# Loading Wq in one transfer instead of two, with the order of the lead-in written anew

## The chip, the cores and the metric

One core of one Trainium2 chip. The time is the device time of one execution in microseconds (us); a kernel's time is the median of several executions. Besides the times there is one profiled execution, whose trace gives the start and length of each instruction on TensorE (PE, its weight loads PEld), VectorE (DVE), ScalarE (ACT), GpSimd (POOL) and the queue of SyncE (SP), which issues the DMAs here.

## The reference

A layer norm, then a sliding dilated attention (32 heads of 16, window 8, dilation 2) and a gated feed-forward side by side, added to the input. S = 2048 rows, D = 512, Df = 1376, all bf16.

```python
xn  = layernorm(x)                                # over the 512 columns
qkv = xn @ wqkv                                   # 512 x 1536: q, k, v
k, v at positions s, s-2, ..., s-14               # masked where negative
o   = softmax(q . k * 16**-0.5) . v               # per head, 8 positions
att = o @ wo
h   = gelu(xn @ w_gate) * (xn @ w_up)             # 512 x 1376 each
out = x + att + h @ w_down
```

## The kernel before

The rows are worked in four blocks of 512 (b = 0 to 3), each of four tiles of 128 rows (t = 0 to 15). Input loads bring pairs of tiles (p = 0 to 7): ld_x0 and ld_x1 as two loads of 128 rows each, the others as one load of 256 rows. Everything stays in SBUF; all weights are loaded once.

The program is a graph of named tasks (`G.task`, with the items that each reads and writes) and an order per engine written out by hand in `ORDER`, a string of task names for each of pe, act, dve, pool and sp. `schedule` walks these orders and gives buffers and PSUM banks (8 of them, pool `ps`) to the tasks, and `assign_sync` sets semaphore waits for what a task reads, overwrites or needs freed. Each engine then executes its list strictly in order: a task that waits holds up all behind it on its engine. On SP that holds for DMA issues: an issue that waits for an event keeps later ones from being issued. The durations in `PARAMS` and in the tasks (`nbytes` too) serve only that walk through the orders; they emit nothing.

What happens in the lead-in, for block 0:

- ld_x0_0, ld_x0_1, Wq in two halves (ld_wq0: rows 0 to 255, ld_wq1: rows 256 to 511, 256 KB each, L652), ld_x1_0, ld_wk, ld_x1_1, ld_wv (L646, 512 KB each), ld_x2, ld_x4, ld_x3, then ld_wg0 and ld_wu0 (L664, 1280 KB each), where ld_wg0 is made to wait until ld_wk has landed. ld_x3 and ld_x5 wait for a slot of XIN that the transposes of pair 0 and pair 1 on TensorE free.
- Norms: statistics (bnst, bnag), square root (sq, on ScalarE), reciprocal (rstd), sub and norm, for tiles 0 to 7 on VectorE. Tile 1 has its sums on ScalarE (sx1, negm1, sxx1, sq1).
- Transposes of block 0 on TensorE (tpx, tpy), evicted to xnT by evx (ScalarE) and evy (VectorE, half of tiles 0 and 1). For block 1 they are DMA transposes: trx2_0, trx2_1, trx3_0 and trx3_1 (L864), tiles 4 to 7, each after the norm of its tile (norm4 to norm7).
- Q of tiles 0 and 1: mma0_t takes the first two of the four slices of 128 rows of Wq (they are in ld_wq0) and mmb0_t the last two (ld_wq1), both L970. Then K of tile t is mmt1_t, Q of tiles 2 and 3 mmt0_t (L956), V mmv (L1014); evicted by evq0, evk0, evv0 on ScalarE.
- Feed-forward of block 0: fg0_j and fu0_j (L1259: Wg and Wu), evicted by gelu0_j and uev0_j. The last 96 columns lie in Wt, loaded by ld_wt0, ld_wt1, ld_wt2 (L671).
- Attention of block 0: products q.k on VectorE (pr0_0, pr0_1, L1070), summed (pa0), reduced per head on TensorE by er0_3 (L1106, a part of the feed-forward with Wt, and L1113), masked (L1136), evicted by lc0 (L1142), exponent, and so on. Block 1's products are mm1_w_g_0 (w = 0, 1, 2 for q, k, v; L1039); the first, mm1_0_0_0, needs all four DMA transposes of block 1.

The lines of the load of Wq, as they are before:

```python
if i == 0:
    for h in range(2):
        ...
                Wqkv[:, 2 * h:2 * h + 2, 0:512],
                A_wqkv[256 * h:256 * h + 256, 0:512].rearrange("(k p) n -> p k n", p=128))
        t_w = G.task("sp", "ld_wq%d" % h, 0, mk(), wr=[(I_wq, ("q", h))], ...)
```

Of the kernel before, what the change touches and what calls it, by code (L numbers as in the profile page):

```python
# [96 lines left out]
class Graph:  # L97
# [250 lines left out]
    def report(self):  # L348
# [14 lines left out]
ORDER = {  # L363
    "pe":
        "warm0 warm1 warm2 warm3 warm4 warm5 warm6 warm7 warm8 warm9 tpx0_0 tpy0_0 warm10 warm11 warm12 "
        "warm13 warm14 mma0_0 tpx0_1 tpy0_1 mmb0_0 mma0_1 mmb0_1 mmt1_0 tpx1_0 mmt1_1 mmt1_2 tpx1_1 mmt0_2 "
        "mmv0_1 mmt1_3 mmt0_3 mmv0_0 mmv1_0 fg0_0 fg0_1 fg0_2 fg0_3 fu0_0 fg0_4 fu0_1 fu0_2 fu0_3 mm1_0_0_0 "
        "fu0_4 mm1_1_0_0 fg0_5 mm1_1_1_0 fu0_5 er0_3 mm1_0_1_0 fg0_6 mm1_2_3_0 fg1_0 mm1_0_2_0 mm1_1_2_0 "
        "mm1_0_3_0 mm1_1_3_0 fu1_0 fg0_7 fu0_6 fu0_7 fg1_1 fu1_1 fg0_10 fg0_8 fg1_2 fu1_2 fg1_3 mm1_2_2_0 "
        "fu1_3 fg0_9 fg1_4 mmv1_1 fu1_4 fu0_8 fu0_9 er1_3 fg1_5 mm1_2_0_0 fg1_6 fu1_5 fg1_7 fg1_8 fu1_6 fg1_9 "  # L370
# [6 lines left out]
        "fg3_9 fu3_8 fu3_9 acca8 accb8 accd11 acca12 accd15_1 accd9 accb12 accd13 accd14_0 accd10 accd15_0 "  # L377
        "accw13 accw15_1 accw15_0 accw12 accd14_1 accw14_0 accw14_1 accd15_2 accw15_2",
    "act":
        "c_tbl sx1 sq0 negm1 sxx1 evx0_0 sq1 evx0_1 sq2 evq0_0 evq0_1 evx1_0 sq3 evk0_1 evk0_0 bnst8 evx1_1 "  # L380
        "evk0_2 sq4 evq0_2 bnst9 sq6 evk0_3 ve8 evq0_3 vp8 bnag8 evv0_1_0 bnag9 evv0_0_1 sub9 gelu0_1 bnst10 "
        "bnst11 gelu0_0 uev0_0 ve10 gelu0_3 vp10 evv0_0_0 uev0_3 va8 gelu0_2 vb8 evq1_0_0 bnag10 evk1_0_0 "
        "uev0_4 uev0_2 bnag11 uev0_1 va10 halo1 bnst12 evk1_1_0 vb10 lc0 evq1_1_0 uev0_5 gelu0_5 gelu0_6 "
        "gelu0_4 exp0 evq1_2_0 evv1_3_0 evq1_3_0 bnst13 evk1_3_0 ln0 d5_0 evk1_2_0 gelu1_0 sub10 uev0_6 "
        "gelu1_1 uev1_1 uev1_0 sub8 uev0_10c ve12 uev0_10a uev0_10b uev0_7 norm8 gelu0_10 gelu0_8 sub11 "
# [10 lines left out]
        "uev2_9 uev3_6 gelu3_6 gelu3_7 gelu2_8 uev3_10a gelu3_10 uev3_7 uev3_9 gelu3_9 fe8 gelu3_8 uev3_8 "  # L396
        "fe11 fe9 fe10 fe13 fe12",
    "dve":
        "c_wdz bnst0 bnag0 sub0 rstd0 norm0a norm0b mean1 sub1 evy0_0 rstd1 norm1a norm1b evy0_1 bnst2 bnag2 "
        "sub2 rstd2 norm2 bnst3 bnag3 sub3 rstd3 norm3 bnst4 bnst5 bnag4 bnag5 bnst6 bnst7 bnag6 rstd4 sub5 "  # L400
        "bnag7 sub4 sub7 norm5 rstd6 norm4 sub6 norm7 norm6 pr0_1 pr0_0 pa0 h0_1 mask h0_0 rstd8 d1a_0 d1b_0 "
        "d1c_0 d2_0 pr1_0 d4a_0 rstd10 d4b_0 d4c_0 h0_2 d6_0 pr1_1 h1_0 pa1 h0_10 pb1 h0_3 pv0_1 d1a_1 h1_1 "
        "h0_4 d1b_1 pv0_0 d1c_1 h1_2 d2_1 h1_3 pw0_1 d4a_1 pw0_2 d4b_1 pz0 d4c_1 pr2_0 rstd12 d6_1 pr2_1 "
        "h1_10 fin3 h1_4 pa2 fin0 rstd14 pb2 pv1_0 d1a_2 fin1 d1b_2 pv1_1 d1c_2 d2_2 pw1_1 d4a_2 d4b_2 h2_1 "
# [4 lines left out]
        "c_ones c_onef c_id c_vnpad c_idb c_eps c_mhalf c_e8a c_e8b c_e8c c_e8d c_ktpad c_mask0 c_mask1 c_utz "  # L409
        "sq8 sq10 sq12 sq14",  # L410
    "sp":
        "ld_x0_0 ld_x0_1 ld_wq0 ld_wq1 ld_x1_0 ld_wk ld_x1_1 ld_wv ld_x2 ld_x4 ld_x3 ld_wg0 ld_wu0 ld_x5 "
        "ld_wt0 trx3_0 trx3_1 trx2_1 trx2_0 ld_x6 ld_wt1 ld_wt2 ld_wd0 ss0_0 ss0_3 ss0_1 ss0_2 ld_wd1 ld_x7 "
        "sl0_3 ld_wo sl0_2 ldxr1 ldxr3 sl0_0 trx4_0 sl0_1 trx5_1 trx5_0 trx4_1 ss1_1 ss1_0 ss1_2 ss1_3 sl1_0 "
        "ldxr0 trx6_1 sl1_1 sl1_2 sl1_3 ldxr2 trx7_1 trx6_0 trx7_0 ss2_2 ss2_3 ldxr8 sto1 ss2_1 ldxr9 ss2_0 "
        "sto3 sl2_0 sl2_1 ldxr4 ldxr11 sl2_3 sl2_2 ldxr7 ldxr5 sto4 ldxr15 sto2 ldxr14 ss3_1 ss3_2 ldxr6 "
        "ss3_3 ss3_0 ldxr12 ldxr10 ldxr13 sto0 sl3_1 sl3_0 sl3_2 sl3_3 sto7 sto5 sto11 sto8 sto9 sto6 sto10 "
        "sto15_1 sto13 sto15_0 sto12 sto14_0 sto14_1 sto15_2",
}


# [16 lines left out]
def bass_parallel_sum__sliding_local_dilated__glu_gated_geglu__prompt_kernel(nc, A_x, A_wqkv, A_wo, B_x, B_w_gate, B_w_up, B_w_down, out, dbg=None, cfg=None):  # L438
# [43 lines left out]
    with contextlib.ExitStack() as es:  # L482
        block = es.enter_context(nc.Block())

        def sb(name, shape, dt):
            return es.enter_context(nc.sbuf_tensor(name, shape, dt))

        Wqkv = sb("Wqkv", [128, 4, 1536], BF)
# [11 lines left out]
        mask = sb("mask", [32, 2, 4, 16], F32)  # L500
# [43 lines left out]
        G = Graph()  # L544
# [20 lines left out]
        I_wq = Item("Wqkv")  # L565
# [51 lines left out]
               prio=PC2)  # L617
        G.task("pool", "c_vnpad", 0.15, lambda e: e.memset(VN[:, VNI[0].slot, :, 0:16], 0.0), wr=[(VNI[0], "pad")],
               prio=PC2)
# [12 lines left out]
        for i, wn in enumerate(WARM[0] + WARM[1]):  # L632
# [6 lines left out]
            t_w = G.task("pe", "warm%d" % i, wn / 1200 if i < len(WARM[0]) else d_mm(wn), mk_w(), wr=[it_warm], prio=-400, mode="f")  # L639
# [4 lines left out]
        for i, nm in enumerate(("q", "k", "v")):  # L644
            def mk(i=i):
                return lambda e: e.dma_start(  # L646
                    Wqkv[:, :, i * 512:(i + 1) * 512],
                    A_wqkv[:, i * 512:(i + 1) * 512].rearrange("(k p) n -> p k n", p=128))
            if i == 0:
                for h in range(2):  # L650
                    def mk(h=h):
                        return lambda e: e.dma_start(  # L652
                            Wqkv[:, 2 * h:2 * h + 2, 0:512],
                            A_wqkv[256 * h:256 * h + 256, 0:512].rearrange("(k p) n -> p k n", p=128))
                    t_w = G.task("sp", "ld_wq%d" % h, 0, mk(), wr=[(I_wq, ("q", h))], prio=-958 + 0.1 * h,
                                 nbytes=480 * 1024)
                continue
            t_w = G.task("sp", "ld_w" + nm, 0, mk(), wr=[(I_wq, nm)],
                         prio=(-958, -957.5, -898)[i], nbytes=512 * 1024)
            t_ld["w" + nm] = t_w  # L660
        I_wt = Item("Wt")
        for (nm, Wx, I_w, src) in (("g", Wg, I_wg, B_w_gate), ("u", Wu, I_wu, B_w_up)):
            def mk(Wx=Wx, src=src):
                return lambda e: e.dma_start(Wx[:, :, :], src[:, 0:1280].rearrange("(k p) n -> p k n", p=128))  # L664
            t_w = G.task("sp", "ld_w%s0" % nm, 0, mk(), wr=[I_w], prio=R_WG + (nm == "u"), nbytes=1280 * 1024)
            t_w.deps.add(t_ld["wk"])
            t_ld[nm] = t_w
        for (i, src, c0, c1, o) in ((0, B_w_gate, 1280, 1376, 32), (1, B_w_up, 1280, 1312, 0),
                                    (2, B_w_up, 1312, 1376, 128)):
            def mk(src=src, c0=c0, c1=c1, o=o):  # L670
                return lambda e: e.dma_start(Wt[:, :, o:o + c1 - c0],  # L671
                                             src[:, c0:c1].rearrange("(k p) n -> p k n", p=128))
            t_w = G.task("sp", "ld_wt%d" % i, 0, mk(), wr=[(I_wt, i)], prio=R_WG + 2 + i, nbytes=2 * (c1 - c0) * 1024)
            G.order_after(t_w, t_ld["u"])
            t_ld["u"] = t_w
        t_w = G.task("sp", "ld_wd0", 0, lambda e: e.dma_start(
            Wd[:, 0:10, :], B_w_down[0:1280, :].rearrange("(j p) n -> p j n", p=128)),
            wr=[(I_wd, 0)], prio=R_WD, nbytes=2000 * 1024)
# [4 lines left out]
        t_w = G.task("sp", "ld_wo", 0, lambda e: e.dma_start(Wo[:, :, :], A_wo.rearrange("(p q) n -> p q n", q=4)),  # L683
                     wr=[I_wo], prio=R_WD + 2, nbytes=512 * 1024)
# [8 lines left out]
        for p in range(NP):  # L693
# [55 lines left out]
            for ts in (((2 * p,), (2 * p + 1,)) if b == 0 else ((2 * p, 2 * p + 1),)):  # L749
                t, n = ts[0], len(ts)  # L750
# [715 lines left out]
```

## Time and profile before

| | us |
|---|---|
| median of 3 runs | 184.42 (184.01 to 185.21) |
| the profiled execution | 184.79 |
| its span, first to last instruction | 182.7 |
| TensorE busy / idle in the span | 177.2 / 5.5 |
| VectorE busy | 169.0 |
| ScalarE busy | 131.8 |

The granted TensorE clock is full throughout. Three kinds of view are read below. The chain of waits goes back from the last instruction to what released each step, and shows in order of time which engine or DMA set the end. A timeline lists the instructions of one engine by start time and, in brackets, how long the engine stood idle before and what ended that. For SP, a row is the time in which an issue occupied the queue, not the transfer itself; a transfer's time to landing is listed apart, counted from the start of its issue:

| load | issued at | us to landing | KB |
|---|---|---|---|
| ld_x0_0 | 0.80 | 2.1 | 128 |
| ld_wq0 | 1.71 | 3.2 | 256 |
| ld_wq1 | 2.19 | 3.4 | 256 |
| ld_x1_0 | 2.70 | 3.4 | 128 |
| ld_wk | 3.21 | 6.0 | 512 |
| ld_x1_1 | 3.69 | 6.0 | 128 |
| ld_wv | 4.23 | 6.9 | 512 |
| ld_wg0 | 9.27 | 8.9 | 1280 |
| ld_wu0 | 9.68 | 11.7 | 1280 |
| ld_x5 | 12.65 | 9.5 | 256 |
| trx3_0, trx3_1 | 16.97, 18.62 | 5.9, 4.8 | |
| trx2_1, trx2_0 | 20.96, 22.27 | 3.1 | |
| ld_x6 | 23.66 | 2.9 | 256 |
| ld_wt1, ld_wt2 | 24.22, 24.77 | 2.6, 4.2 | 32, 64 |

### The profile page before, as it was taken

The page shows a single profiled execution, that of the slowest core. Times are in us where ns is not written, and L with a number is a line of the kernel's source. Part 1 is how long each engine was busy: PE and PEld are TensorE (multiplying, and loading weights), DVE is VectorE, ACT ScalarE, POOL GpSimd, SP SyncE. Part 2 cuts the span into 40 slices and gives each one's busy share as a digit, 9 for nine tenths or more (in the row PEclk, how much of TensorE's full clock was granted, in tenths as well). Part 3 has the DMA queues.
Part 4 walks back from the last instruction along what each step waited for, and adds up shares of the span by engine and source line. Part 5 has one row for each costly group of instructions (what it writes and reads, how often), then busy time and mean ns, then how long its engine had stood idle before and what let it go on. Part 6 is the DMA issues. An engine that isn't in the chain of part 4 may idle for free.

```text
span 182.7 us, 2780 instructions
## 1 busy us (share of the span) xinstructions
PE 177.2 (97%) x1060; PEld 90.5 (50%) x1060; DVE 169.0 (92%) x157; ACT 131.8 (72%) x270; POOL 17.4 (10%) x23
## 2 busy tenths in 40 slices
PE   7799999999999999999999999999999999999994
PEld 2598445444454445444445444444444444454574
DVE  3779997699999999989999999999999999999953
ACT  5569989999999999999387598844268679411030
POOL 6000006200000000974000000000000000000000
PEclk9999999999999999999999999999999999999999
DMA  4999968001794200002572000528105058410113
GB/s 149 299 365 397 141 136 287 2 0 33 171 292 103 57 4 0 0 0 59 144 221 40 0 0 0 125 64 255 47 0 148 1 112 249 127 57 4 57 44 99
DMA packets 26236, 19.60 MB, mean 107 GB/s; under 512 B 13840, under 2 KB 23024, under 8 KB 26224
## 3 DMA queue, kind: packets, MB, share of 16 engines
q1 hardware_dynamic: 26224, 19.44, 39.2%
q8 instruction: 8, 0.13, 0.3%
q14 instruction: 4, 0.03, 0.1%
HBM read 14.71 MB, written 3.15 MB: 98 GB/s over the span
## 4 chain that ended last, share of the span: by engine, by line
PE 55%; ACT 22%; DMA 8%; DVE 6%; POOL 5%; issue 2%; SPq 1%; DVEq 0%
PE PS L1351 23%; PE PS L1259 21%; PE PS L1039 9%; DMA Wg<-in_B_w_gate_dram 5%; POOL sq L803 5%; ACT UU L1276 4%; ACT GG L1269 4%; DMA Wqkv<-in_A_wqkv_dram 3%; DVE UNI L1070 2%; ACT XIN L824 2%; DVE UNI L1082 2%; ACT L1164 1%; ACT EX L1165 1%; ACT PB L1142 1%; ACT KT L1050 1%
## 5 line engine op out<-in xcount | busy, mean ns | idle before, releaser
L1351 PE MATMUL PS<-Wd,HT 128*128 128x512 bf16 (+2 forms) x209 | 40.7, 345 | 0.0
L1259 PE MATMUL PS<-xnT,Wg 128*128 128x512 bf16 x160 | 39.3, 379 | 0.3 <-DMA Wg<-in_B_w_gate_dram 0.3
L1259 PE MATMUL PS<-xnT,Wu 128*128 128x512 bf16 x160 | 39.4, 379 | 0.0
L1221 DVE TENSOR_TENSOR UNI<-VN,PT 128x8192 f16<-128x8192 bf16 x8 | 35.4, 4420 | 0.0
L1070 DVE TENSOR_TENSOR UNI<-QT,KT 128x8192 f16<-128x8192 bf16 x8 | 35.3, 4419 | 0.0
L1039 PE MATMUL PS<-xnT,Wqkv 128*128 128x512 bf16 x144 | 34.7, 379 | 0.1
L1351 PEld LDWEIGHTS PS<-Wd,HT 128*128 128x128 bf16 x209 | 19.7, 98 | 19.4
L1276 ACT ACTIVATE UU<-PS 128x512 bf16<-128x512 f32 x40 | 23.2, 607 | 6.4 <-PE PS L1259 6.3
L1384 ACT ACTIVATE OB<-PS 128x512 bf16<-128x512 f32 x14 | 8.3, 595 | 23.2 <-PE PS L1351 23.1
L1259 PEld LDWEIGHTS PS<-xnT,Wg 128*128 128x128 bf16 x160 | 15.1, 98 | 19.8 <-ACT UU L1276 0.8
L1259 PEld LDWEIGHTS PS<-xnT,Wu 128*128 128x128 bf16 x160 | 15.6, 98 | 18.6 <-ACT KT L1050 0.3
L1039 PEld LDWEIGHTS PS<-xnT,Wqkv 128*128 128x128 bf16 x144 | 16.2, 114 | 15.6 <-ACT UT L1314 0.6
L1269 ACT ACTIVATE GG<-PS 128x512 bf16<-128x512 f32 x40 | 23.0, 608 | 0.5 <-DVE HT L1283 0.4
L803 POOL TENSOR_TENSOR sq<-ve,mhalf 128x2 bf16<-128x2 f32 x4 | 14.6, 3642 | 68.3 <-ACT ve L799 68.3
L1082 DVE TENSOR_TENSOR UNI<-UNI 128x8192 f16<-128x8192 f16 x4 | 17.7, 4420 | 0.0
L1230 DVE TENSOR_TENSOR UNI<-UNI 128x8192 f16<-128x8192 f16 x4 | 17.7, 4420 | 0.0
L1351 PE MATMUL PS<-Wo,OT 128*128 128x512 bf16 (+2 forms) x76 | 16.3, 345 | 0.0
L1283 DVE TENSOR_TENSOR HT<-GG,UU 128x1024 bf16<-128x1024 bf16 x20 | 13.5, 684 | 0.2 <-ACT UU L1276 0.2
L1351 PEld LDWEIGHTS PS<-Wo,OT 128*128 128x128 bf16 x76 | 6.9, 98 | 6.4 <-DVE OT L1241 0.5
L1236 DVE TENSOR_TENSOR UNI<-UNI 128x4096 f16<-128x4096 f16 x4 | 9.1, 2286 | 0.0
L1050 ACT ACTIVATE KT<-PS 128x512 bf16<-128x512 f32 x12 | 7.2, 601 | 2.0 <-PE PS L1039 2.0
L1050 ACT ACTIVATE VN<-PS 128x512 bf16<-128x512 f32 x12 | 7.2, 597 | 1.0 <-PE PS L1039 0.9
(99 smaller groups left out, 179.2 us busy)
## 6 DMA issues: line engine op xcount, KB each, us to landing
PT<-pt_scratch SPq DMA_DIRECT2D x16, 256.0 KB, 4.0
out_dram<-OB SPq DMA_DIRECT2D x14, 128.0 KB, 1.8
XIN<-in_A_x_dram SPq DMA_DIRECT2D x12, 128.0 KB, 2.7
XIN<-in_A_x_dram SPq DMA_DIRECT2D x6, 256.0 KB, 6.8
Wg<-in_B_w_gate_dram SPq DMA_DIRECT2D x1, 1280.0 KB, 8.9
Wu<-in_B_w_up_dram SPq DMA_DIRECT2D x1, 1280.0 KB, 11.7
Wd<-in_B_w_down_dram SPq DMA_DIRECT2D x1, 1280.0 KB, 7.2
Wqkv<-in_A_wqkv_dram SPq DMA_DIRECT2D x2, 512.0 KB, 6.5
```

The costliest lines, as they stand in the source:

```text
L803: "pool", "sq%d" % t, 5.0, lambda e, t=t, n=n: e.tensor_tensor(out=sq[:, t:t + n], in0=ve[:, t:t + n], in1=mhalf[:, 0:n], op=ALU.pow),
L1039: ins = e.matmul(PS[:, 512 * it.slot:512 * it.slot + 512], lhsT=wcols(which, kt, g), rhs=xnT[:, itx.slot, kt, :], start=(kt == 0), stop=(k ...
L1050: return e.activation(out=o, in_=PS[:, 512 * it.slot:512 * it.slot + 512], func=ACTF.Identity, scale=(QSC, 1.0, 1.0)[which])
L1070: return lambda e: e.tensor_tensor(out=UNI[:, it.slot:it.slot + 2, :, :], in0=bass.AP(QT, (itq.slot * 4 + 2 * h) * 512, [[NQT * 4 * 512, 1 ...
L1082: return lambda e: e.tensor_tensor(out=UNI[:, i0.slot:i0.slot + 2, :, :], in0=UNI[:, i0.slot:i0.slot + 2, :, :], in1=UNI[:, i1.slot:i1.slo ...
L1221: return lambda e: e.tensor_tensor(out=bass.AP(UNI, ito.slot * 4096, [[NUNI * 4096, 128], [2048, 4], [512, 4], [1, 512]]), in0=bass.AP(VN, ...
L1230: return lambda e: e.tensor_tensor(out=UNI[:, i0.slot:i0.slot + 2, :, :], in0=UNI[:, i0.slot:i0.slot + 2, :, :], in1=UNI[:, i1.slot:i1.slo ...
L1259: ins = e.matmul(PS[0:M, 512 * it.slot:512 * it.slot + 512], lhsT=Wx[:, kt, j * 128:j * 128 + M], rhs=xnT[:, itx.slot, kt, :], start=(kt = ...
L1269: return lambda e: e.activation(out=GG[:, ito.slot, q, :], in_=PS[:, 512 * it.slot:512 * it.slot + 512], func=ACTF.Gelu_apprx_tanh)
L1276: return lambda e: e.activation(out=UU[:, ito.slot, q, :], in_=PS[:, 512 * it.slot:512 * it.slot + 512], func=ACTF.Identity)
L1283: return lambda e: e.tensor_tensor(out=HT[:, ito.slot, j - 1:j + 1, :], in0=GG[:, ig.slot, :, :], in1=UU[:, iu.slot, :, :], op=ALU.mult)
L1351: ins = e.matmul(PS[:, 512 * it.slot:512 * it.slot + CW], lhsT=(OT[:, ito.slot, q, ti * 128:(ti + 1) * 128] if kind == "o" else HT[:, ith. ...
```

## The change

Wq comes in one load of all 512 rows, in the form that Wk and Wv have already. The load writes both parts of the item that mma and mmb read, so all four of mma0_0, mma0_1, mmb0_0 and mmb0_1 now wait for the whole.

```diff
-            if i == 0:
-                for h in range(2):
...
-                            Wqkv[:, 2 * h:2 * h + 2, 0:512],
-                            A_wqkv[256 * h:256 * h + 256, 0:512].rearrange("(k p) n -> p k n", p=128))
-                    t_w = G.task("sp", "ld_wq%d" % h, 0, mk(), wr=[(I_wq, ("q", h))], prio=-958 + 0.1 * h,
-                                 nbytes=480 * 1024)
-                continue
-            t_w = G.task("sp", "ld_w" + nm, 0, mk(), wr=[(I_wq, nm)],
-                         prio=(-958, -957.5, -898)[i], nbytes=512 * 1024)
+            t_w = G.task("sp", "ld_w" + nm, 0, mk(), wr=[(I_wq, (nm, 0)), (I_wq, (nm, 1))] if i == 0 else [(I_wq, nm)],
+                         prio=(-958, -957.5, -898)[i], nbytes=(900 if i == 0 else 512) * 1024)
```

The orders differ in their first parts alone: TensorE's 27th to 43rd task, ScalarE's 6th to 43rd, VectorE's 14th to 44th, SP's first 22. All tasks behind these stand as before (GpSimd's order is the same throughout). The parts that differ, cut where they are equal; the line breaks of the strings are moved:

```diff
 pe:   ... mmt1_0 tpx1_0 mmt1_1
-      mmt1_2 tpx1_1 mmt0_2 mmv0_1 mmt1_3 mmt0_3 mmv0_0 mmv1_0 fg0_0 fg0_1 fg0_2 fg0_3 fu0_0 fg0_4 fu0_1 fu0_2 fu0_3
+      mmt0_2 tpx1_1 mmt1_2 mmv0_1 mmt0_3 mmt1_3 mmv0_0 mmv1_0 fg0_0 fg0_1 fg0_2 fg0_3 fu0_0 fu0_1 fu0_2 fu0_3 fg0_4
       mm1_0_0_0 fu0_4 mm1_1_0_0 fg0_5 mm1_1_1_0 fu0_5 er0_3 ...
 act:  c_tbl sx1 sq0 negm1 sxx1
-      evx0_0 sq1 evx0_1 sq2 evq0_0 evq0_1 evx1_0 sq3 evk0_1 evk0_0 bnst8 evx1_1 evk0_2 sq4 evq0_2 bnst9 sq6 evk0_3
-      ve8 evq0_3 vp8 bnag8 evv0_1_0 bnag9 evv0_0_1 sub9 gelu0_1 bnst10 bnst11 gelu0_0 uev0_0 ve10 gelu0_3 vp10
-      evv0_0_0 uev0_3 va8 gelu0_2
+      sq1 evx0_0 evx0_1 sq2 evq0_0 evq0_1 evx1_0 sq3 evk0_0 evk0_1 bnst8 evx1_1 bnst9 sq4 evk0_2 ve8 sq6 evq0_2
+      vp8 evq0_3 evk0_3 bnag8 evv0_0_1 bnag9 evv0_1_0 sub9 gelu0_0 bnst10 bnst11 uev0_0 va8 gelu0_3 gelu0_1 ve10
+      gelu0_2 vp10 evv0_0_0 uev0_3
       vb8 evq1_0_0 bnag10 ...
 dve:  ... rstd1 norm1a norm1b
-      evy0_1 bnst2 bnag2 sub2 rstd2 norm2 bnst3 bnag3 sub3 rstd3 norm3 bnst4 bnst5 bnag4 bnag5 bnst6 bnst7 bnag6
-      rstd4 sub5 bnag7 sub4 sub7 norm5 rstd6 norm4 sub6 norm7 norm6 pr0_1 pr0_0
+      bnst2 bnag2 evy0_1 sub2 rstd2 norm2 bnst3 bnag3 sub3 rstd3 norm3 bnst5 bnst4 bnst6 bnag5 bnag4 bnag6 bnst7
+      sub4 bnag7 rstd4 sub6 sub7 rstd6 norm4 norm7 sub5 norm6 norm5 pr0_0 pr0_1
       pa0 h0_1 mask ...
 sp:   ld_x0_0 ld_x0_1
-      ld_wq0 ld_wq1 ld_x1_0 ld_wk ld_x1_1 ld_wv ld_x2 ld_x4 ld_x3 ld_wg0 ld_wu0 ld_x5
-      ld_wt0 trx3_0 trx3_1 trx2_1 trx2_0 ld_x6 ld_wt1 ld_wt2
+      ld_wq ld_x1_0 ld_wk ld_x1_1 ld_wv ld_x2 ld_x4 ld_x3 ld_wg0 ld_wu0 ld_x5
+      trx3_1 ld_wt0 trx3_0 ld_wt1 ld_wt2 trx2_1 trx2_0 ld_x6
       ld_wd0 ss0_0 ...
```

With the orders the PSUM banks that many tasks use change their numbers, since `schedule` hands them out as it goes.

## The prediction

> **What bounds the kernel now.** First the page's list of busy time, which says that TensorE has almost no room:
>
> ```profile
> PE 177.2 (97%) x1060; PEld 90.5 (50%) x1060; DVE 169.0 (92%) x157; ACT 131.8 (72%) x270; POOL 17.4 (10%) x23
> ```
>
> Of the span of 182.7 us, TensorE is idle for 5.5. An edit of the lead-in can win only from the part of those 5.5 us that lies in the lead-in, and loses whatever idle time it adds. Next the chain of waits in order of time (start, length, what):
>
> ```profile
> 3.21 6.05 DMA Wqkv<-in_A_wqkv_dram
> ...
> 9.27 8.87 DMA Wg<-in_B_w_gate_dram
> 18.14 0.05 issue
> 18.19 7.94 PE PS L1259 x36
> 26.14 0.86 PE PS L1039 x4
> ...
> 31.86 0.89 PE PS L1113 x16
> ```
>
> The Wk load (ld_wk) lands at 9.26, Wg lands at 18.14, and from 18.19 TensorE runs without a gap to the logits er0_3 (L1113); VectorE's mask at 32.85 and ScalarE's lc0 at 33.17 take over from there. Further on the chain is ScalarE to 72.6, GpSimd's power (L803) to 81, and TensorE from 95 to 180. So a shift of TensorE between 18 and 32 us goes into the end one for one. Then TensorE's own timeline, for where its idle time is:
>
> ```profile
> 6.61 1.53 PE L970 MATMUL PS<-xnT,Wqkv 128*128 128x128 bf16 x24
> 9.30 1.08 PE L956 MATMUL PS<-xnT,Wqkv 128*128 128x128 bf16 x16 [1.17 <-DMA Wqkv<-in_A_wqkv_dram]
> ...
> 18.19 3.63 PE L1259 MATMUL PS<-xnT,Wg 128*128 128x512 bf16 x16 [0.28 <-DMA Wg<-in_B_w_gate_dram]
> ```
>
> The Q products of the first two row tiles (L970, what the split of Wq feeds) end at 8.13. TensorE then waits 1.17 us for Wk and later 0.28 us for Wg. Last the SP queue, which issues every transfer:
>
> ```profile
> 1.71 0.94 SPq L652 DMA_DIRECT2D Wqkv<-in_A_wqkv_dram  x2
> 2.70 0.47 SPq L702 DMA_DIRECT2D XIN<-in_A_x_dram  x1
> 3.21 0.43 SPq L646 DMA_DIRECT2D Wqkv<-in_A_wqkv_dram  x1
> ...
> 9.27 0.37 SPq L664 DMA_DIRECT2D Wg<-in_B_w_gate_dram  x1
> ...
> 13.06 0.47 SPq L671 DMA_DIRECT2D Wt<-in_B_w_gate_dram  x1
> 16.97 6.57 SPq L864 DMA_TRANSPOSE xnT<-XIN  x4
> 23.66 0.51 SPq L708 DMA_DIRECT2D XIN<-in_A_x_dram  x1
> 24.22 1.05 SPq L671 DMA_DIRECT2D Wt<-in_B_w_up_dram  x2
> ```
>
> One issue costs about 0.5 us; a DMA transpose of a row tile costs 1.60, 2.30, 1.27 and 1.27 us for the four in turn.
>
> **What the Trainium skill says.** "DMA: Bandwidth & Descriptors", section "Queues, rings and completion order": each DMA engine consumes a queue's descriptors in ring order. The trace agrees: in the list of issues with their time to landing, all come from SP and land in order (halves of Wq at 4.9 and 5.6, x1_0 at 6.1, Wk at 9.2, x1_1 at 9.7, Wv 11.1, Wg 18.14, Wu 21.4). The same page, "Why a DMA increments its semaphore by 16 and not by 1": the engines finish independently, and only the full count says that all landed. The trace fits: from 20 to 22 us only 31 GB/s move, yet Wu lands at 21.4 and x5 (issued at 12.65) at 22.15, so stragglers decide. [...] The first 128 KB x load takes 2.1 us from issue to landing, so one load in place of two saves no wait by itself; it saves an issue.
>
> **The change part by part.**
>
> (1) One issue less. x1_0, Wk, x1_1, Wv, x2 and x4 are issued 2.70 - 2.19 = 0.51 us earlier. The bytes are the same, and the queue is in order. The stretches show 209, 336, 209 and 262 GB/s for the microseconds from 3 to 7, and 354 to 400 from 7 to 18. So the stream is not full early on, and some of the 0.51 can be won, but only if late issues cause those dips; DMA engines were still 73% to 96% busy in them. Bounds for Wk's landing: 0.5 earlier to 0.2 later (one load of 512 rows has not been seen at this place; the same shape, Wk, took 6.0 us behind a backlog). I take 0.25 earlier. Everything behind keeps its place in the stream, so Wg also lands 0.25 earlier: 17.89. TensorE's work from Wk to Wg is 17.91 - 9.30 = 8.6 us without a gap, ready at 17.66. fg0_0 then starts at about 17.94: **-0.25** (bounds -0.5 to +0.2).
>
> (2) The Q products. mma0_0 starts at 5.58, after its eviction evx0_0 ends at 5.52; now it needs all of Wq. In order, the last byte of Wq comes no later than that of the second half, which landed at 5.6; nothing is lost there. sq1 moves ahead of evx0_0 on ScalarE (0.29 us later for mma0_0); bnst2 and bnag2 move ahead of evy0_1 on VectorE (evy0_1, which ended at 7.10, now ends at about 6.42 + 0.69 + 0.24 + 0.29 = 7.64; mmb0_1, which waits for it, is 0.45 us long and ends near 8.15). All of this is covered by the 1.17 us in which TensorE waits for Wk: **0**. If that cover shrinks by 0.25, 0.9 remains.
>
> (3) The other swaps to 18 us (mmt0_2 before mmt1_2, mmt0_3 before mmt1_3, the norms, evk and evq, the bnst) are the same instructions in another order under the same bounds: TensorE full from 9.30, VectorE from 11.66. pr0 still starts after the last eviction and norm, near 16.9, and VectorE waits 1.79 us for er0_3 before the mask, which covers it: **0** (-0.1 to +0.2).
>
> (4) On SP the four transposes for block 1 trade places with the Wt loads. The first of them, trx3_0, waited 3.4 us for norm6, the last norm, which ended at 16.94; now trx3_1 comes first and waits for norm7, with sub5, norm6, norm5 behind it: 3 x 0.26 = 0.78 us earlier, 16.2. Queued behind that wait is now ld_wt0, which the chain needs only at 31.3. Then: trx3_1 to 17.80, wt0 to 18.32, trx3_0 to 20.67, wt1 and wt2 (1.05) to 21.77, trx2_1 to 23.09, trx2_0 issued at 23.13 in place of 22.27: 0.86 later. In the trace it took 3.1 us to land: 25.4 before, 26.2 now. mm1_0_0_0, the first product of block 1, waits for all four; its first weight load was at 25.8. So 0.4 us of slack is used and TensorE stalls about **+0.4**. Bounds: 0, if the second transpose takes 1.27 instead of 2.30 (its excess lies beside Wu's tail); +1.7, if wt2, now ahead of trx2_1 in the ring, takes the 4.2 us that it took before: it lands at 21.27 + 4.2 = 25.5, and the last two transposes, which followed the second by 0.7 and 2.0 us (landings 23.4, 24.1, 25.4), end at 27.5 in place of 25.8. Behind mm1_0_0_0 in TensorE's order stand fu0_4 and er0_3, for which the mask and lc0 wait.
>
> (5) ld_x6 is issued at about 24.4 in place of 23.66, needed by bnst12 at 31.63 (landed 26.6): 0. wd0 keeps its time. fg0_4 moves behind fu0_3 and gelu0_0, uev0_0 lead on ScalarE; mm1_0_0_0 still comes tenth (after nine times 0.86), and the PSUM banks that fu0_3 and fg0_4 wait for are freed by gelu0_0 (22.3) and uev0_0 (24.1), against 24.2 and 25.1: 0.
>
> Sum: -0.25 + 0.4 = +0.15. The profiled execution took 184.79 us (span 182.7 and 2.1 around it), which is 0.37 above the median of 184.42. So 184.9 for it, and about **184.6** for the median.
>
> **The rivals.** A, the sum above: 184.6, own range 184.0 to 185.3, chance 0.48. B, the slower one: the transposes become the bound at mm1_0_0_0. It decides from the point where trx2_0 lands after 25.8; with a stall of 1.0 to 1.7 there and nothing won in (1) the median is 185.4 to 186.1, say 185.7, and 186.3 with Wk 0.2 late as well. For it: 0.86 us of added SP time against 0.4 of slack. Against: the 2.30 us one may shrink. Chance 0.30. C, the stream was bound by issues: the whole 0.5 us reaches TensorE and the transposes are in time, 183.9; for it the dips to 209 GB/s, against it the engines' busy share; 0.16. D, the change does not do what it says: the single load lands no differently and everything hides, 184.4; 0.06. Should Wq land past about 6.6 us, the cover of (2) is gone and each us more costs one; nothing in the ring order speaks for it, and it is within the ends.
>
> **How the numbers follow.** 1% is 1.84 us, about what a measurement of this kernel can tell from no change. Faster by that needs 1.84 of the 1.17 + 0.28 us waited for loads and then some: 0.07 for what I overlook. Slower by that needs the far end of B, or a knock-on later: 0.17. Within: 0.76. The range takes A, C and most of B: 183.6 to 186.2.
>
> **What would show it.** Wk's landing below 9.2 and the first Wg product near 17.9 show (1); no new idle time before L970 beyond 1.2 us in all shows (2); a wait of TensorE at the first L1039 near 26 us, for the transposes, shows (4). I am wrong if fg0_0 starts past 18.4, or if new idle time appears after 32 us, where the order is unchanged.

## The result, and the profile after

| | before | after |
|---|---|---|
| median of 18 runs each, us | 184.08 (183.42 to 187.02) | 183.31 (183.1 to 183.84) |
| ratio after / before | | 0.9957, 95% interval 0.9942 to 0.9973 |
| the profiled execution, us | 184.79 | 183.42 |
| its span, us | 182.7 | 181.3 |
| Wk landed at, us | 9.2 | 7.73 |
| first product of Wg, fg0_0, us | 18.19 | 16.52 |

The change makes the kernel 0.77 us faster, 0.4%: less than the 1% that the forecast called distinguishable, but the interval leaves out 1. The forecast (184.6, up 0.15) had the sign wrong, and the time lies below its range. The rows below the ratio come from one execution each and need care: the profiled execution of before lies 0.7 us above the median of its 18 runs, that of after 0.1 above. So of the 1.4 us between the two profiles only about half is the change. Landings are the start of the issue plus the listed time to landing, and good to 0.05 us.

The busy list of after:

```profile
PE 176.5 (97%) x1043; PEld 90.7 (50%) x1060; DVE 168.7 (93%) x157; ACT 131.7 (73%) x270; POOL 18.5 (10%) x23
```

17 matmul records are missing (1043 of 1060), so its 176.5 can't be set against the 177.2 of before; VectorE and ScalarE were busy for the same time as before to 0.3 us. The difference has to be looked for in when things start. TensorE's timeline of after (start, length, what; the Q products, the first K product, Wg, Wu, and the first product of block 1):

```profile
5.94 0.64 PE L961 MATMUL PS<-xnT,Wqkv 128*128 128x128 bf16 x8
...
6.64 1.61 PE L961 MATMUL PS<-xnT,Wqkv 128*128 128x128 bf16 x24
8.09 1.06 PE L947 MATMUL PS<-xnT,Wqkv 128*128 128x128 bf16 x16
...
16.74 3.40 PE L1250 MATMUL PS<-xnT,Wg 128*128 128x512 bf16 x15
19.98 3.62 PE L1250 MATMUL PS<-xnT,Wu 128*128 128x512 bf16 x16
...
24.58 1.05 PE L1030 MATMUL PS<-xnT,Wqkv 128*128 128x512 bf16 x4
```

(Line numbers are those of before less 9.) The Q products end about where they ended before (8.14 there, 8.25 here, by start and length; neighbouring rows overlap a little). But the bracket behind the first K product is gone: before it said that TensorE had been idle 1.17 us for Wk; now K follows Q at once. The 0.28 us for Wg is gone too. The group of Wg has 15 of its 16 records: the first is missing, and fg0_0 began 3.46 us (the distance in the profiles whose first Wg record is there) before Wu's 19.98, at 16.52. The SP queue of after:

```profile
1.71 0.43 SPq L646 DMA_DIRECT2D Wqkv<-in_A_wqkv_dram  x1
2.18 0.51 SPq L693 DMA_DIRECT2D XIN<-in_A_x_dram  x1
2.73 0.43 SPq L646 DMA_DIRECT2D Wqkv<-in_A_wqkv_dram  x1
...
15.14 1.31 SPq L855 DMA_TRANSPOSE xnT<-XIN  x1
16.50 0.57 SPq L662 DMA_DIRECT2D Wt<-in_B_w_gate_dram  x1
17.12 1.29 SPq L855 DMA_TRANSPOSE xnT<-XIN  x1
18.46 1.90 SPq L662 DMA_DIRECT2D Wt<-in_B_w_up_dram  x2
20.40 2.50 SPq L855 DMA_TRANSPOSE xnT<-XIN  x2
```

x1_0 and Wk are issued 0.5 us earlier than before, as forecast. But Wk lands 1.5 us earlier. Where the rest comes from can be read in the stretches of time (from:to, length, busy time of PE, PEld, DVE, ACT and POOL with counts, clock, busy share of the DMA engines, which passes 1 in places, and GB/s). First before, then after, each from the start to 7 us and the microseconds from 5 to 6 and 6 to 7:

```profile
0.00:7.00 7.00, 5.62 (x39) 2.85 (x39) 3.62 (x14) 4.21 (x11) 2.85 (x19) 1.00 0.62 183
...
5.00:6.00 1.00, 1.00 (x16) 0.82 (x15) 0.82 (x5) 0.71 (x4) 0.00 (x0) 1.00 0.84 209
6.00:7.00 1.00, 0.93 (x16) 0.69 (x14) 0.62 (x3) 0.38 (x1) 0.00 (x0) 1.00 0.90 262
```

```profile
0.00:7.00 7.00, 6.12 (x38) 3.14 (x39) 3.96 (x14) 4.14 (x11) 2.85 (x19) 1.00 0.69 212
...
5.00:6.00 1.00, 0.96 (x10) 0.72 (x11) 0.88 (x6) 0.85 (x4) 0.00 (x0) 1.00 1.07 347
6.00:7.00 1.00, 1.00 (x19) 1.00 (x20) 1.00 (x3) 0.27 (x1) 0.00 (x0) 1.00 1.10 372
```

By 7 us after has moved 7 x (212 - 183) = 203 KB more. At the 354 GB/s that before reaches in the next microsecond this is 0.57 us. It comes from 5 to 7 us: there the stream of before sags although everything up to Wv had been issued by then. The rest of the 1.5 us is bytes of later loads that had moved before Wk was complete: when Wk landed, before had moved 2,070 KB (225 GB/s to 9.2 us) and after 1,732 (224 to 7.73), and 338 KB at 354 GB/s are 0.95 us. This is a reckoning in bytes and not a cause. The second part varies from execution to execution: it was 1,857 KB in a second profile of before (211 GB/s to 8.8 us) and 1,958 in a second one of after (235 to 8.33). The first part stays: the mean to 7 us is 179 to 183 GB/s in both profiles of before and 207 to 215 in all three of after.

Last the chain of waits of after, where it passes the lead-in:

```profile
20.40 1.20 SPq L855
21.59 0.04 issue
21.64 2.90 DMA xnT<-XIN
24.53 0.05 issue
24.58 1.05 PE PS L1030 x4
25.63 0.86 PE PS L1250 x4
```

Wk and Wg, which began the chain of before, are not in it. It goes through the last of the DMA transposes of block 1, which lands at 24.53 and lets mm1_0_0_0 start at 24.58: the wait that step (4) foresaw.

### The profile page after: what moved, and what is told of

Read it like the earlier page. It is cut to its first block, busy times and chain, and to the rows that moved or that the text cites. A ratio compares the mean times of both kernels' runs of the same rounds, so it can differ in the third digit from the quotient of the medians.

```text
span 181.3 us, 2762 instructions
## 1 busy us (share of the span) xinstructions
PE 176.5 (97%) x1043; PEld 90.7 (50%) x1060; DVE 168.7 (93%) x157; ACT 131.7 (73%) x270; POOL 18.5 (10%) x23
## 4 chain that ended last, share of the span: by engine, by line
DVE 54%; ACT 21%; PE 10%; POOL 5%; DMA 5%; issue 4%; SPq 1%; DVEq 0%
DVE UNI L1212 14%; DVE UNI L1061 9%; DVE UNI L1221 7%; POOL sq L794 5%; ACT GG L1260 4%; DVE UNI L1073 4%; ACT UU L1267 4%; DVE UNI L1227 4%; DVE HT L1274 3%; DMA XIN<-in_A_x_dram 3%; PE PS L1342 3%; PE PS L637 2%; DVE OT L1232 2%; DVE OB L1380 2%; DMA xnT<-XIN 2%
## 5 line engine op out<-in xcount | busy, mean ns | idle before, releaser
L1250 PE MATMUL PS<-xnT,Wu 128*128 128x512 bf16 x156 | 38.9, 379 | 0.2
L1250 PE MATMUL PS<-xnT,Wg 128*128 128x512 bf16 x155 | 38.7, 379 | 0.4 <-issue 0.2
L794 POOL TENSOR_TENSOR sq<-ve,mhalf 128x2 bf16<-128x2 f32 x4 | 15.7, 3916 | 65.8 <-ACT ve L790 65.8
```

Source lines behind the costliest of these rows:

```text
L794: "pool", "sq%d" % t, 5.0, lambda e, t=t, n=n: e.tensor_tensor(out=sq[:, t:t + n], in0=ve[:, t:t + n], in1=mhalf[:, 0:n], op=ALU.pow),
L1250: ins = e.matmul(PS[0:M, 512 * it.slot:512 * it.slot + 512], lhsT=Wx[:, kt, j * 128:j * 128 + M], rhs=xnT[:, itx.slot, kt, :], start=(kt = ...
```

## The experiments

**A yardstick.** In 14 of the 17 profiles of this study the span is the start of fg0_0 plus 164.5 us, within 0.2; in after and late_issue2, where TensorE waits for the transposes, 164.8 and 165.0; in split_wk_first 164.9, where TensorE waits 0.35 us for ScalarE before 31.55, at the head of er0_3. So nearly all of a run's difference can be read in the lead-in:

| run | mean GB/s to 7 us | GB/s, 5 to 6 us | Wk landed | first K product | fg0_0 | span | median of runs |
|---|---|---|---|---|---|---|---|
| before | 183 | 209 | 9.2 | 9.30 | 18.19 | 182.7 | 184.08 |
| before_again | 179 | 121 | 8.8 | 8.87 | 17.32 | 181.8 | (one run) |
| split_new | 181 | 143 | 8.9 | 8.96 | 17.41 | 181.9 | 184.02 |
| join_only | 216 | 358 | 8.63 | 8.69 | 17.14 | 181.6 | 183.23 |
| after | 212 | 347 | 7.73 | 8.09 | 16.52 | 181.3 | 183.31 |
| after_again | 215 | 363 | 8.33 | 8.79 | 17.21 | 181.7 | 183.36 |
| after_third | 207 | 376 | 7.92 | 8.35 | 16.77 | 181.3 | 183.54 |
| trx_first | 214 | 382 | 7.63 | 8.05 | 16.47 | 181.0 | 183.42 |
| trx_first2 | 210 | 384 | 8.33 | 8.75 | 17.18 | 181.7 | 183.49 |
| tiny_dma | 201 | 288 | 8.09 | 8.17 | 17.12 | 181.6 | 183.44 |
| tiny_dma2 | 208 | 335 | 8.19 | 8.20 | 16.65 | 181.3 | 183.44 |
| late_issue | 187 | 276 | 9.9 | 9.91 | 18.36 | 182.9 | 183.92 |
| late_issue2 | 193 | 277 | 8.38 | 8.42 | 17.18 | 182.1 | 184.00 |
| late_more | 157 | 134 | 9.48 | 9.49 | 18.48 | 183.1 | 184.42 |
| x0_join | 217 | 309 | 8.73 | 8.75 | 17.20 | 181.7 | 183.84 |
| split_wk_first | 208 | 313 | 8.29 | 8.32 | 18.08 | 183.0 | 185.36 |
| wq1_act | 193 | 258 | 10.0 | 11.37 | 20.37 | 184.9 | 185.53 |

The runs of before measured beside them had medians of 183.85 (with join_only, split_new, trx_first), 183.86 (tiny_dma, late_issue, x0_join, after_again), and 184.04 (all others but after). A single profile differs from the next of the same kernel by up to 0.9 us, so verdicts rest on medians, and a profile says what happened in one execution. That execution can be an extreme: it is the slowest of its runs for join_only, late_issue, after_again and wq1_act, and the fastest for trx_first.

**Load or orders?** join_only has after's load of Wq with before's orders, split_new the two halves with after's orders, and before_again is before unchanged.

```diff
 join_only (before, with the load of after), sp:
-      ld_x0_0 ld_x0_1 ld_wq0 ld_wq1 ld_x1_0
+      ld_x0_0 ld_x0_1 ld_wq ld_x1_0
 split_new (after, with the loads of before), sp:
-      ld_x0_0 ld_x0_1 ld_wq ld_x1_0
+      ld_x0_0 ld_x0_1 ld_wq0 ld_wq1 ld_x1_0
```

> The kernel before, unchanged, profiled a second time. In its first profile Wk landed at 9.2 us, with 209 to 262 GB/s in the microseconds 5 to 7, and TensorE waited 1.17 us for it. Theory 'split' (two halves of Wq slow the stream behind them in every execution): Wk again lands at 9.0 to 9.4 and the dip at 5 to 7 us is there. Theory 'issue' (only the 0.5 us of the second issue): the same picture, Wk at 9.0 to 9.4, since nothing is changed. Theory 'chance' (the dip comes and goes from execution to execution and the first profile caught a bad one): Wk lands well earlier, 7.9 to 8.8, and the span is 181.3 to 182.2 instead of 182.7.

> Only the load of Wq is joined; all orders stay those of before, with ld_wq in the place of the two halves. Theories 'split' and 'issue' (the gain is the load's): ratio to before 0.995 to 0.998, Wk landing under 8.5 us ('split': near 7.7 as in the changed kernel; 'issue' alone: 0.5 earlier than before's). Theory 'order' (the new orders give the gain and the load nothing): ratio 0.999 to 1.001.

> The orders of the changed kernel, but Wq in two halves. Theories 'split' and 'issue': no gain, ratio 0.999 to 1.002, Wk lands about as late as in before. Theory 'order': the whole gain stays, ratio 0.995 to 0.997.

join_only: 0.9966 (0.9957 to 0.9976). split_new: 1.0007 (0.9998 to 1.0017). The whole gain is the load's; the orders alone are worth nothing either way. The two kernels' stretch from 5 to 6 us, join_only first:

```profile
5.00:6.00 1.00, 0.88 (x12) 0.65 (x13) 0.85 (x5) 0.85 (x4) 0.00 (x0) 1.00 1.05 358
```

```profile
5.00:6.00 1.00, 0.64 (x7) 0.58 (x8) 0.90 (x4) 0.97 (x4) 0.00 (x0) 1.00 0.74 143
```

In these two the sag goes with the split. join_only's timeline of TensorE still has Wk as the bound, but with a shorter wait than the 1.17 of before:

```profile
8.69 1.08 PE L947 MATMUL PS<-xnT,Wqkv 128*128 128x128 bf16 x16 [0.41 <-DMA Wqkv<-in_A_wqkv_dram]
```

before_again landed Wk at 8.8 rather than 9.2, as the expectation had it for chance, but with a deeper sag:

```profile
5.00:6.00 1.00, 1.00 (x16) 0.80 (x15) 0.82 (x5) 0.73 (x4) 0.00 (x0) 1.00 0.80 121
```

So the sag is there in both executions of before, and part of what the first two profiles show is spread between executions. The wait for Wg is such a part: before_again has none, its fg0_0 comes 8.45 us behind the first K product against 8.89 in before.

**The transposes.** trx_first puts them ahead of the two loads of Wt that the change had put before them; trx_first2 repeats it beside after_third, which is after unchanged.

```diff
-      trx3_1 ld_wt0 trx3_0 ld_wt1 ld_wt2 trx2_1 trx2_0 ld_x6
+      ld_wt0 trx3_1 trx3_0 trx2_1 trx2_0 ld_x6 ld_wt1 ld_wt2
```

> The changed kernel with the SP order behind ld_x5 put to ld_wt0, the four transposes, ld_x6, ld_wt1, ld_wt2 (wt1 and wt2 no longer ahead of the last two transposes). My reading of step 4 (the transposes are late by about 0.3 us at mm1_0_0_0 in the changed kernel): the gap before the first product of block 1 closes, the time is 0.2 to 0.4 us below the changed kernel's 183.31, ratio to before 0.993 to 0.995. Rival (the gap is covered later or Wt becomes late at er0_3): 183.2 to 183.5, ratio 0.995 to 0.997.

> The same kernel as trx_first, now timed in one call with the changed kernel. If the 0.3 us that TensorE waited for the transposes in the changed kernel's first profile is the usual case, it is 0.15 to 0.3 us below the changed kernel (ratio of the two 0.998 to 0.999). If that wait comes only in executions where the first Wg product starts early, the two are equal within 0.1 us.

> The changed kernel again, beside trx_first2. Wk lands at 7.6 to 8.5, ratio to before 0.995 to 0.9975. In every profile so far the span is the start of the first Wg product plus 164.5 us, and 0.3 more where TensorE waits for the transposes; the same is expected here to 0.1 us.

In trx_first the wait is gone: fg0_0 starts 0.05 us earlier than in after, mm1_0_0_0 0.34 earlier, at 24.24 in place of 24.58. TensorE's timeline of trx_first there, with the end of the feed-forward products ahead of it and no bracket:

```profile
23.38 1.03 PE L1250 MATMUL PS<-xnT,Wg 128*128 128x512 bf16 x4
24.24 1.03 PE L1030 MATMUL PS<-xnT,Wqkv 128*128 128x512 bf16 x4
```

That is 0.29 us of stall in the profile, and the span of trx_first, 181.0, is 0.3 shorter. In the medians it can't be seen: trx_first 0.9972 (0.9958 to 0.9987), trx_first2 0.9958 (0.9945 to 0.9972) beside after_third 0.9976 (0.996 to 0.9992). The stall comes in one of the three profiles of after: in after_again, where fg0_0 starts at 17.21, and in after_third (16.77) mm1_0_0_0 starts 7.77 us behind it as in before_again. What decides is how long after fg0_0 the last transpose lands: 8.0 us in after, 7.4 and 7.7 in the other two. An early fg0_0 is not needed: late_issue2 below has fg0_0 at 17.18, its last transpose lands 8.15 us behind it, and TensorE waits:

```profile
25.37 1.06 PE L1032 MATMUL PS<-xnT,Wqkv 128*128 128x512 bf16 x4 [0.25 <-DMA xnT<-XIN]
```

No version was found that is certain to beat after.

**Is it the number of loads or the time of issue?** The joined load lets x1_0 and Wk be issued 0.5 us earlier, and it is also another form. tiny_dma adds a load of 16 KB into scratch behind ld_wq, which takes the freed place on SP. late_issue gives the time back by a wait on a GpSimd task, without another DMA: x1_0 leaves at 2.72, Wk at 3.08. x0_join joins ld_x0_0 and ld_x0_1 instead and leaves Wq split, so that everything else comes 0.4 us earlier. after_again is after unchanged.

```diff
 tiny_dma (after), and "ld_wq ld_tiny ld_x1_0" on sp:
+        G.task("sp", "ld_tiny", 0, lambda e: e.dma_start(SUB[0:16, :], x2[0:16, :]), wr=[I_su], nbytes=16 * 1024)
 late_issue (after), t_e8d being the task c_e8d:
+                    if (p, t2) == (1, 0):
+                        G.order_after(t_x, t_e8d)
 x0_join (before), and "ld_x0" for "ld_x0_0 ld_x0_1" on sp:
+            if p == 0:
+                G.task("sp", "ld_x0", 0, lambda e, it=it_x: e.dma_start(
+                    XIN[:, it.slot, :, :], x2[0:256, :].rearrange("(t q) d -> q t d", q=128)),
+                    wr=xp(it_x, 0, 0) + xp(it_x, 0, 1), nbytes=256 * 1024)
```

> The changed kernel with one more DMA between Wq and x1_0, of 16 KB into a scratch buffer: the second issue is back, the joined load stays. Theory 'count' (each DMA takes a share in series of the way from issue to data, so one DMA more puts off all behind it): the stream drops again to 120 to 210 GB/s in the microsecond 5 to 6, Wk lands at 8.5 to 9.2, ratio to before 0.999 to 1.001. Theory 'form' (two loads of 256 rows slow what follows, the number of issues does not matter): no dip at 5 to 6 us, Wk lands at 7.7 to 8.3, ratio 0.995 to 0.997.

> The changed kernel with x1_0, and all issues behind it, held until GpSimd's c_e8d has ended, so that x1_0 is issued at about 2.7 us as in the kernel before: the half microsecond of issue time is given back, with no further DMA. Theory 'issue' (the 0.5 us at SP is what counts): dip at 5 to 6 us, Wk lands at 8.8 to 9.2, ratio to before 0.998 to 1.001. Theories 'count' and 'form': no dip, Wk at 7.7 to 8.2, ratio 0.995 to 0.997.

> The kernel before, Wq still in two halves and all orders as they were, but the two loads of x0 (128 rows each) joined into one of 256 rows: one DMA less ahead of Wk, at another place. Theory 'count' or 'issue': the dip at 5 to 6 us goes, Wk lands at 7.7 to 8.5, ratio to before 0.994 to 0.998. Theory 'form': the dip stays, Wk at 8.5 to 9.2 (0.5 earlier at most by the issue), ratio 0.997 to 1.002; the first tile of x comes about 0.4 us later, which the wait for Wk covers.

> The changed kernel, unchanged, timed and profiled a second time beside these. If its early Wk is not chance: no dip at 5 to 6 us, Wk lands at 7.6 to 8.6 (join_only had 8.6), ratio to before 0.995 to 0.997. If it is chance: Wk at 8.8 or later in this profile.

Measured: tiny_dma 0.9978 (0.9962 to 0.9995), late_issue 1.0001 (0.9982 to 1.002), x0_join 0.9997 (0.9987 to 1.0007), after_again 0.9966 (0.9952 to 0.998). The late issue by a wait takes the gain back, as far as an interval of 0.4% can tell. The late issue by a small load hardly does, though x1_0 and Wk then leave at 2.73 and 3.19, as in the split kernel. The profile of late_issue is a poor witness: in that execution x0_1, which is issued ahead of the wait, landed 2.9 us after its issue in place of 2.1, and the Q products started at 6.72. And x0_join, which has a good stream, gains nothing. Its timeline of TensorE says why:

```profile
6.33 0.81 PE L974 MATMUL PS<-xnT,Wqkv 128*128 128x128 bf16 x8
...
8.75 1.08 PE L960 MATMUL PS<-xnT,Wqkv 128*128 128x128 bf16 x16
```

Tile 0 came with the joined load at 3.6 us instead of 2.9, so the Q products started at 6.33 instead of 5.6, and K follows them at 8.75 with no wait for Wk. One bound was swapped for another; the expectation had taken the later tile as covered.

after_again also has the Q products as its bound, from another cause. Its chain of waits and its timeline of TensorE:

```profile
1.71 4.83 DMA Wqkv<-in_A_wqkv_dram
```

```profile
6.67 0.61 PE L961 MATMUL PS<-xnT,Wqkv 128*128 128x128 bf16 x8 [0.66 <-DMA Wqkv<-in_A_wqkv_dram]
7.34 1.61 PE L961 MATMUL PS<-xnT,Wqkv 128*128 128x128 bf16 x24
8.79 1.06 PE L947 MATMUL PS<-xnT,Wqkv 128*128 128x128 bf16 x16
```

The load at 1.71 is Wq: in this execution it landed at 6.5 (5.8 in after), TensorE waited 0.66 us for it, and Q, not K, sets the start of everything behind.

**More of the delay, and the half on another queue.** late_more makes x1_0 wait for a later GpSimd task, so that it leaves at 3.40 and Wk at 3.78. wq1_act is split_new with the second half of Wq issued by ScalarE; in ScalarE's order the issue stands behind the table load and ahead of the first sums (sx1).

```diff
 late_more (after): t_e8d is the task c_mask1
 wq1_act (split_new):
+                    t_w.on_act = h == 1
```

> As late_issue, but x1_0 and all behind it are held until c_mask1 ends, about 3.4 us, 1.2 us later than in the changed kernel and 0.7 later than before. Theory 'issue', with Wk's landing following its issue one for one: Wk lands 0.6 to 0.8 later than in before's usual execution, at 9.4 to 9.7, ratio to before 1.002 to 1.005. Rival (a fixed price once the stream runs dry behind Wq, whatever the delay): ratio 0.999 to 1.001.

> The orders of the changed kernel with Wq in two halves (as in split_new), but the second half is issued from ScalarE's queue at about 2.3 us, where ScalarE has nothing to do, so that x1_0 and Wk are issued from SP as early as in the changed kernel (2.18 and 2.73). Theory 'issue' (what counts is when the loads behind Wq are issued): no dip at 5 to 6 us, Wk lands at 7.6 to 8.4, ratio to before 0.995 to 0.998. Theory 'form' (two loads of 256 rows slow what follows): dip at 5 to 6 us, Wk at 8.7 to 9.2, ratio 0.999 to 1.002.

late_more: 1.0025 (1.0011 to 1.004), so 0.88 us behind after_third, measured beside it, for an issue 1.22 us later; late_issue was 0.56 behind after_again for 0.54. Its stretches and its chain:

```profile
5.00:6.00 1.00, 0.76 (x10) 0.50 (x11) 0.93 (x6) 0.88 (x4) 0.00 (x0) 1.00 0.61 134
6.00:7.00 1.00, 1.00 (x18) 1.00 (x19) 0.36 (x2) 0.24 (x1) 0.00 (x0) 1.00 0.74 217
```

```profile
3.40 0.33 SPq L693
3.78 5.66 DMA Wqkv<-in_A_wqkv_dram
9.46 8.97 DMA Wg<-in_B_w_gate_dram
```

A joined Wq with a late Wk has the sag of the split kernel, and the chain of before (Wk, then Wg) is back. So the joined form by itself doesn't keep the stream going.

wq1_act, 1.0066 (1.0037 to 1.0094), tells nothing of the question, since the half was not issued at 2.3 us as intended. The first lines of ScalarE's timeline:

```profile
0.80 1.28 ACT L627 ACT_TABLE_LOAD   x1 [0.80 <-PEq L1452]
1.07 0.46 ACTq L652 DMA_DIRECT2D Wqkv<-in_A_wqkv_dram  x1
...
5.05 0.63 ACT L732 ACTIVATE XR<-XIN 128x512 bf16<-128x512 bf16 x1 [2.75 <-DMA XIN<-in_A_x_dram]
```

ScalarE's queue issued the half at 1.07 us, ahead of x0_1 (1.25), and x0_1 then landed 3.8 us after its issue in place of 2.1. ScalarE waited 2.75 us for it, and the Q products started at 7.55. The Trainium skill, "DMA: Bandwidth & Descriptors", section "Issuing engines are not separate DMA queues", says that DMAs from different engines interleave on the same 16 DMA engines; the late x0_1 agrees with that. How much of it is due to the second queue is not shown: this is the slowest execution of wq1_act, and x0_1 took 2.9 us in late_issue, where SP issues every load.

**Early issue with the halves kept.** split_wk_first puts Wk before x1_0, so that Wk leaves at 2.69 with Wq still split. tiny_dma2 and late_issue2 repeat the two that disagreed.

```diff
 split_wk_first (before)
-  sp: ld_wq0 ld_wq1 ld_x1_0 ld_wk ld_x1_1      pe: mmt1_0 tpx1_0 mmt1_1
+  sp: ld_wq0 ld_wq1 ld_wk ld_x1_0 ld_x1_1      pe: mmt1_0 mmt1_1 tpx1_0
```

> The kernel before with Wq in two halves, but Wk issued ahead of x1_0 (at 2.70, as early as the 2.73 of the changed kernel), and on TensorE the K product of tile 1 ahead of the transpose of tile 2, which now comes later. Theory 'issue' (what counts is when Wk is issued): Wk lands at 7.7 to 8.4, the stream holds over 300 GB/s in the microsecond 5 to 6. Theory 'form' (two loads slow what follows them): Wk lands at 8.5 or later, the stream drops to 120 to 220 GB/s. The time is secondary, as x1_0 lands later: ratio 0.996 to 1.000 under 'issue', 0.999 to 1.004 under 'form'.

> The kernel of tiny_dma again, beside late_issue2. If issuing late by a further DMA costs less than issuing late by a wait: ratio to before again 0.997 to 0.9985, and Wk near 8.1. If the first run was chance: 0.999 to 1.001, Wk at 8.5 or later.

> The kernel of late_issue again. Its first profile had Wk at 9.9 and x0_1, ahead of the wait, landing in 2.9 us instead of 2.1, so it may have been a bad execution. Expected now, under 'issue': Wk at 8.3 to 8.9, ratio 0.998 to 1.000. If the wait is really worse than a DMA in its place: ratio 0.9995 to 1.002.

split_wk_first: the stretch from 5 to 6 us, and TensorE's timeline.

```profile
5.00:6.00 1.00, 1.00 (x13) 0.84 (x14) 0.82 (x5) 0.86 (x4) 0.00 (x0) 1.00 0.94 313
```

```profile
8.32 1.98 PE L956 MATMUL PS<-xnT,Wqkv 128*128 128x128 bf16 x32
...
11.64 1.08 PE L956 MATMUL PS<-xnT,Wqkv 128*128 128x128 bf16 x16 [0.69 <-ACT xnT L914]
```

With the halves kept, Wk landed at 8.29 and 313 GB/s moved from 5 to 6 us. So the split by itself doesn't make the sag either; the last line shows what the order costs: tile 2 comes late (x1_0 landed near 8.6), TensorE waits 0.69 us for its eviction, and the time is 1.0064 (1.0045 to 1.0083). tiny_dma2 is 0.9975 (0.9964 to 0.9986), late_issue2 0.9992 (0.9979 to 1.0006): the disagreement repeats, with 0.56 us between the medians after 0.48 the first time. The intervals overlap in each pair, so it is the repetition that speaks for it. The streams differ too: up to 7 us the two with the small load moved 201 and 208 GB/s, the two with the wait 187 and 193.

Put in the order of the stream's rate, leaving out three runs whose tile or Q came late by their edit (x0_join, split_wk_first, wq1_act), the ratios to before fall in line, though each rate is that of one execution and each ratio that of many: 157 GB/s gives 1.0025; 181 (split_new) 1.0007; 187 and 193 give 1.0001 and 0.9992; 201 to 216 give 0.9957 to 0.9978.

## Why the prediction was wrong

The forecast said +0.15 and 0.77 less was measured: 0.92 us. A further 0.34 of the distance from 184.6 to 183.31 is the level it started from, a median of three runs at 184.42 where eighteen gave 184.08; that part of the miss is chance.

**Step (1) failed: the size of "one issue less".** It took 0.25 us with an end at 0.5, since Wk is issued 0.5 us earlier. Measured: Wk 1.5 us earlier in the first pair of profiles, and fg0_0 1.67; over all profiles of the two kernels Wk landed at 9.2 and 8.8 before, at 7.7, 8.3 and 7.9 after, 1.0 earlier on average. In the medians, with the yardstick of 164.5 us and the 2.1 us around the span, fg0_0 stands at 184.08 - 2.1 - 164.5 = 17.5 before. After it is 183.31 - 166.6 = 16.7, or 16.4 if the stall of (4) is there. The term is therefore -0.8 to -1.1 us. Two sentences of the step are at fault. The bound took it that a landing can't move by more than its issue; Wk's moved by two to three times as much, and the bytes lost in the sag from 5 to 7 us are alone worth 0.57 us. And the step held the busy share of the DMA engines against a gain: "still 73% to 96% busy". The pair of lines above says that this was no evidence: 209 GB/s at 0.84, 347 at 1.07; before_again moved 121 GB/s at a share of 0.80. The GB/s column alone (209 and 262, against 354 in the next microsecond) showed that a quarter to two fifths of the stream's rate was there to be had. The rates from 7 to 18 us were misread too, 317 to 402 and not 354 to 400, but nothing rests on that. That fg0_0 waits for Wg was taken from the first profile of before; in before_again and after it doesn't.

**Step (2) held in its number, but not in its cover, nor in its reason.** The Q products end 0.1 later than before, and as long as Wk is later than that they cost nothing. But the step left 0.9 us of cover, and it was all used: with Wk at 7.73 the K products start only when the Q products are through, 0.36 us after Wk. In after_again and after_third 0.46 and 0.43 are lost there in the same way. The step set its alarm at a Wq later than 6.6 us; that was worked out for a Wk at 9.0. After it, Wq at 6.5 already costs (first K product 8.79 against 8.09). The step's reading of the ring order failed as well: it had all of Wq there no later than the second half was, but in the eleven profiles with the joined load it landed at 5.7 to 6.5, and the second half, where SP issued it, at 5.2 to 5.6 in five. The joined load is the later one for Q; only the cover hides it.

**Step (3), the other swaps at 0, held**: split_new has all of them and measures 1.0007 (0.9998 to 1.0017). This covers step (4)'s order in the split kernel too, where it is hidden.

**Step (4): the mechanism as told, the size near.** The stall came at mm1_0_0_0, for the transposes, 0.29 us where 0.4 was forecast. In terms of fg0_0, trx2_0 was issued 5.1 us behind it in place of 4.1, so 1.0 later, against the 1.1 of the forecast (0.86 and the 0.25 by which fg0_0 came earlier); its landing took 2.9 us rather than 3.1. On the way two errors cancelled: the second transpose took 1.29 us and not the 2.30 of before, one of the two ends given, and the two loads ld_wt1 and ld_wt2 held SP for 1.90 and not 1.05. But the stall came in only one of three profiles of after, so the step's +0.4 is no fixed cost, and it stood against a larger gain than the step knew of. Rival B, in which the stall decides, did not happen.

**Step (5), ld_x6 and the PSUM banks at 0, held**: no wait for either stands in after's list of waits. Rival C, the stream bound by issues, came nearest. It put 183.9 against 184.42 and was held to 0.5 us, too; and a late issue is not all of it, since tiny_dma issues x1_0 and Wk as late as before and keeps most of the gain. Rival D is excluded by join_only.

**What is shown and what isn't.** Shown: the gain belongs to the load of Wq and not to the orders; it goes with the sag of the stream behind Wq; a later issue of x1_0 and Wk, by a wait, takes most or all of it back, and a longer wait costs more. Neither the split with an early Wk (split_wk_first 313 GB/s, x0_join 309) nor a late issue by 0.5 us alone (276 to 335) makes the deep sag in the profile taken; both together do (121 to 209), and 1.2 us of delay does (134). Not shown: what in the queue lets the stream sag, why it does so 2 us after the issues, and why half a microsecond lost to a small load costs the stream less than the same lost to a wait.

## What to carry to other kernels

While a stream of loads feeds the first matmuls, look for microseconds in which it moves half of what it moves later, and don't excuse them by the busy share of the DMA engines; here an issue saved ahead of such a sag was worth more than its own 0.5 us. Then work out the next bound before booking the gain: here the cover of 1.17 us was used up and the Q products and the transposes became the last to end. Take a second profile of the kernel before, since its first one was 0.7 us from its median, about as much as the whole effect, and had a wait for Wg that the second has not.

## What the runs showed of the hardware

The rate of a queue that holds issued loads went with what had been issued 2 to 3 us before: with Wk issued at 2.73 the stream moved 347 to 376 GB/s from 5 to 6 us in the runs of after, with two halves ahead and Wk at 3.21 only 121 to 209, although in both Wv and two more loads of x had been issued by 5.9.

The same load differs in its landing by 0.6 to 0.7 us from one execution to the next at equal issue: Wk of after at 7.73, 7.92 and 8.33, Wq at 5.8, 6.1 and 6.5.

A second queue ran ahead of its engine's work: in wq1_act ScalarE issued at 1.07 us, while the table load that stands ahead of that issue ran from 0.80 to 2.08. A load that SP issued 0.2 us later landed 1.7 us later than usual there.

An issue has no fixed price: the small loads ld_wt1 and ld_wt2 held SP for 0.5 us each before and 0.9 each in after, where transposes stood around them, while a DMA transpose held it for 1.2 to 1.3 in after and up to 2.30 before.
